# Other slots for batch 0's casts, statistics, transposes, value products and gMLP steps in a block-sparse attention + gMLP kernel

## The chip, the core and the metric

The kernel runs on one core of a Trainium2 chip. The metric is device time in microseconds of one execution, the median over runs. Five engines work side by side and wait for each other through semaphores: PE (matmuls and transposes), ACT (ScalarE), DVE (VectorE), POOL (GpSimd) and SP, which here only issues DMA transfers. Each engine runs its own instructions strictly in the order of the program.

## What is computed

Attention of 4 batches, 8 heads, 768 positions, head size 64, under a block mask (blocks of 32: neighbours, first and last block, three sampled blocks for each block row), and then a gated MLP over the 512 joined head outputs:

```python
scores = scale * np.matmul(q, k.transpose(0, 1, 3, 2))
scores = np.where(mask, scores, -1000000000.0)
attn = np.exp(scores - np.max(scores, axis=-1, keepdims=True))
attn = attn / (np.sum(attn, axis=-1, keepdims=True) + 1e-09)
x = np.matmul(attn, v)            # joined over heads: (4, 768, 512)
h = np.maximum(x @ w_in, 0.0)     # (4, 768, 1024)
u, v = h[..., :512], h[..., 512:]
v_n = (v - mean(v)) / np.sqrt(var(v) + 1e-06)
v_s = np.einsum('ts,bsd->btd', w_spatial, v_n) + b_spatial[None, :, None]
out = (u * v_s) @ w_out           # (4, 768, 512)
```

## The kernel before

**Slots.** The order of work on every engine is the order of the program, and the program is a loop over slots `s` (L838), written out by hand through tables. In each slot PE first computes one group of scores, and ACT takes the exponential of it into `a_all`. Then come the value products that are due, the functions entered for this slot with `when` (the list `early`, L844 and L850), a number of gMLP matmuls taken from a queue (`run_queue`, by the table `STEPS`, L769 to L772), the functions in `late`, and the statistics in `post` (L853 to L856). Scores have two PSUM buffers, so the group of slot s waits for the exponential of slot s - 2.

**Batch 0 (slots 0 to 35).** Heads go in pairs p = 0 to 3. Each unit u = 0 to 11 (`UNITS`, L422) is a third of the query positions of a pair, or of one head of pair 0 over two thirds, and takes three slots. A score group is four matmuls of 256 columns (L441) and one exponential of 1024 (L446); the value products are three groups e = 0, 1, 2 of eight matmuls (L487), by default in slots 3u+3, 3u+4, 3u+5, with exceptions in `AV_AT` (L832). After the third, `normalize` divides on DVE (`rc`, `xn`, L469 and L470), and `xtr_third` (L527) transposes the result on PE into the same PSUM bank and copies it to `xt` on DVE (L525), by default in slot 3u+7 with exceptions in `XT_AT` (L742).

**Queries and keys.** They are loaded as float32 on SP's queue (`load`), cast to bfloat16 on POOL (`cast`, L136), and in batch 0 transposed on PE into `kq`: `tr_first` (keys and the first third of the queries), `tr_rest` (the other queries), `third` and `second` for pair 0; copies from PSUM go through DVE (L217). `rows` copies mask rows on DVE (L247). Pairs 4 to 15 are transposed by DMA instead (`tr_dma`, L412) into `tt`, and two DVE copies (`split`, L416), one for each head, bring them into `kq`. In slots 36 on, a score group is two matmuls of 384 columns (L454) with an exponential of 768 (L458), and six value matmuls (L505) follow it.

**Weights.** The halves of `moe_w_in` are loaded in eight pieces `w_in_load(u, g)` (u = 0 is the half that gives v, u = 1 the one that gives u) and cast on POOL (`w_in_cast`, L233), interleaved by hand with the casts of queries, keys and values (L329 to L357).

**gMLP.** A v product is four matmuls (L579) with a relu (DVE, L609) and then `norm`: statistics on DVE (L612, L613) and, when a group is complete, the inverse deviation on POOL (L616, L618). A later DVE instruction normalizes (L633), due some steps after. A u product has its relu on DVE in batch 0, on ACT after (L638 to L641). Then come six s products (with `w_spt`), gated on DVE (L647), transposed by DMA, and six o products, copied to `osb` by DVE or ACT (L674, L675) and written out. The products of batches 0 to 2 share two PSUM banks (`moe_tag`), which `tr_first`, `tr_rest` and `xtr_pe` use too: a product can begin when the one before the last is copied out.

```python
qk_unit(*divmod(s, 3))                 # L840, slots below 36
early = at.get(s, [])                  # L844
for u, e in av_at.get(s, []):
    av_unit(u, e)
for f in early:                        # L850
    f()
run_queue(STEPS.get(s))
for f in late.get(s, []):              # L853
    f()
while post:
    post.pop(0)()
```

Of the kernel before, what the change touches and what calls it, by code (L numbers as in the profile page):

```python
# [26 lines left out]
def kernel(  # L27
# [38 lines left out]
    S0 = NT * NG * 3  # L66
    FILL, FILL2, FILL3 = 24, 4, 4

    const = ctx.enter_context(tc.tile_pool(name="const", bufs=1))
# [144 lines left out]
    PL, DV = nc.gpsimd, nc.vector  # L214
# [48 lines left out]
    load(1, "q", cs=C25)  # L263
    w_in_load(0, 0)
    cast(0, "q", PL, H1, C03)
# [5 lines left out]
    cast(0, "v", PL)  # L271
    load(3, "v")


# [55 lines left out]
    load(2, "q", cs=C25)  # L330
    w_in_load(0, 2)
    w_in_load(0, 3)
    load(3, "q", cs=C25)
    w_in_load(1, 0)
    w_in_load(1, 1)
    load(0, "q", cs=C45)
    cast(3, "k", PL)
# [4 lines left out]
    cast(2, "v", PL)  # L342
    cast(1, "q", PL, cs=C25)
    cast(3, "v", PL)
    w_in_cast(0, 1, PL)
    w_in_cast(0, 0, PL)
    w_in_load(1, 3)
    w_in_load(1, 2)
# [4 lines left out]
    w_in_cast(1, 0, PL)  # L353
    w_in_cast(1, 1, PL)
    cast(0, "q", PL, cs=C45)
    w_in_cast(1, 3, PL)
    w_in_cast(1, 2, PL)  # L357

# [213 lines left out]
    def product(n, lhs, rhs, last, done, w=512):  # L572
# [11 lines left out]
        return out  # L584

    VN_AGE, VN_STEP = 9, 2
    post = []

    class Moe:
# [14 lines left out]
        def v_product(self, tcc, grp):  # L604
            def done(ps):
                if self.last:
                    nc.scalar.activation(out=self.vn[:, tcc, :], in_=ps, func=AF.Relu)  # L607
                else:
                    ts(self.vn[:, tcc, :], ps, 0.0, ALU.max)  # L609
                def norm():  # L610
                    stats = work.tile([128, 6], FP32, tag="stats", bufs=2)
                    nc.vector.bn_stats(out=stats, in_=self.vn[:, tcc, :])  # L612
                    nc.vector.bn_aggr(out=self.mv[:, tcc, :], in_=stats)  # L613
                    if tcc % grp == grp - 1:
                        cs = slice(tcc - grp + 1, tcc + 1)
                        nc.gpsimd.tensor_scalar(out=self.std[:, cs], in0=self.mv[:, cs, 1],  # L616
                                                scalar1=1e-6, scalar2=None, op0=ALU.add)
                        nc.gpsimd.tensor_tensor(out=self.rstd[:, cs], in0=self.std[:, cs],  # L618
                                                in1=mhalf[:, cs], op=ALU.pow)
                        self.vn_due.extend((t, self.steps + VN_AGE + VN_STEP * i)  # L620
                                           for i, t in enumerate(range(cs.start, cs.stop)))
                if self.last:
                    norm()
                else:
                    post.append(norm)
# [10 lines left out]
        def u_product(self, tcc):  # L636
            def done(ps):
                if self.b == 0:  # L638
                    ts(self.un[:, tcc, :], ps, 0.0, ALU.max)
                else:  # L640
                    nc.scalar.activation(out=self.un[:, tcc, :], in_=ps, func=AF.Relu)  # L641
# [21 lines left out]
        def o_product(self, tcc):  # L663
# [4 lines left out]
            for i in range(parts):  # L668
                cs = slice(i * w, (i + 1) * w)

                def done(ps, i=i, cs=cs):
                    if i == 0:
                        osb["t"] = work.tile([128, DM], FP32, tag="osb", bufs=6, name="osb")
                    on_act = (tcc + i) % 2 == 0 and (self.last or self.b > 0)  # L674
                    (act_copy if on_act else dve_copy)(osb["t"][:, cs], ps)  # L675
# [53 lines left out]

    ROWS = [(1, 2, 4, qcols(0)), (1, 2, 3, K_), (3, 3, 4, K_), (4, 4, 6, qcols(0)), (6, 4, 6, K_), (8, 6, 8, qcols(0)), (9, 6, 8, K_)]  # L730
    when(0, second)
    when(1, third)
    when(2, lambda: filler(FILL3, psum.tile([128, 512], FP32, tag=moe_tag(), bufs=1, name="wps")))
    when(4, c(tr_first, 1))
    when(7, c(tr_first, 2))
    when(9, c(tr_first, 3, 0, 4))
    when(10, c(tr_first, 3, 4))
    for sl, h0, h1, cs in ROWS:
        when(sl, c(rows, slice(h0, h1), cs))
    for p, sl in ((1, 11), (2, 16), (3, 18), (0, 21)):  # L740
        when(sl, c(tr_rest, p, 2 if p == 0 else 1))
    XT_AT = {1: 13}  # L742
    for u in range(1, len(UNITS)):
# [25 lines left out]
    when(29, lambda: deal(moe[0].in_steps("v2 v3 u2 u3", TC), 14))  # L769
    STEPS = {20: 1, 21: 2, 22: 1, 23: 1, 24: 2, 25: 1, 26: 1, 27: 2, 28: 1, 29: 1, 30: 1, 31: 1, 32: 2, 33: 1, 34: 1, 35: 1, 36: 1, 37: 0, 38: 1, 39: 2, 40: 2, 41: 2}  # L770
    STEPS.update({s: 2 if (s % 2 == 0) == (s < 67) else 1 for s in range(42, 92)})
    STEPS.update({43: 2, 46: 1})  # L772
    when(42, lambda: deal(moe[0].in_steps("v4 v5 u4 u5", TC) + moe[0].rest_steps(),
# [57 lines left out]
    LAG = 7  # L831
    AV_AT = {0: (5, 5, 6), 1: (6, 8, 8)}  # L832
    av_at = {}
# [54 lines left out]
```

## Time and profile before

| | |
|---|---|
| median of 3 runs | 211.81 us (211.35 to 211.96) |
| the profiled execution | 211.57 us, span of its instructions 209.8 us |
| PE | 203.2 us busy, 97%, 2141 matmuls and transposes |
| ACT | 167.8 us, 80%, 220 instructions |
| DVE | 134.2 us, 64%, 295 |
| POOL | 69.3 us, 33%, 108 |
| DMA | 41.97 MB, mean 200 GB/s |

Rows of a timeline read: start in us from the span's start, time to the end of the row's instructions in us, engine, line of the kernel, operation, what it writes <- what it reads, shapes, count, and in brackets the idle time of the engine before it with what ended it. Groups read: line, engine, operation, count, then busy us, mean ns of one, and idle time before with its releasers. A row of the list of DMA issues ends with the median us from issue to landing.

### The profile page before, as it was taken

How to read it: one execution, taken by the hardware profiler on the slowest of the kernel's cores; microseconds unless marked ns; L12 is line 12 of the kernel's file. 1: busy time of each engine (PE TensorE's matmuls, PEld its weight loads, DVE VectorE, ACT ScalarE, POOL GpSimd, SP SyncE). 2: the span in 40 equal slices, each digit the busy share in tenths (PEclk: the TensorE clock that was granted, in tenths of full speed). 3: DMA queues.
4: the chain of work that ended last, by engine and by line, in shares of the span. 5: the costliest groups of instructions: out<-in, count | busy, mean ns of one | idle time of the engine just before them, and what ended most of it. 6: DMA issues, size and time to landing. Idle time of an engine off the chain costs nothing.

```text
span 209.8 us, 5271 instructions
## 1 busy us (share of the span) xinstructions
PE 203.2 (97%) x2141; PEld 127.8 (61%) x2141; DVE 134.2 (64%) x295; ACT 167.8 (80%) x220; POOL 69.3 (33%) x108
## 2 busy tenths in 40 slices
PE   8898999999999999999999999999999999999992
PEld 6687878756666666655556655666556556544441
DVE  6998585989754536584987455386785433476541
ACT  5899899999999999979998888979999787266021
POOL 5683979665563214033442040131020000013000
PEclk9999999999999999999999999999999999999999
DMA  5999899999999999999981497795101324610266
GB/s 149 346 356 311 269 369 283 285 219 292 258 375 213 266 152 291 237 296 355 207 239 38 100 264 176 230 314 88 38 3 25 63 53 98 228 66 0 50 170 230
DMA packets 64295, 41.97 MB, mean 200 GB/s; under 512 B 45184, under 2 KB 59024, under 8 KB 64272
## 3 DMA queue, kind: packets, MB, share of 16 engines
q1 hardware_dynamic: 63696, 41.06, 76.4%
q10 hardware_dynamic: 576, 0.59, 0.8%
q8 instruction: 16, 0.26, 0.5%
q14 instruction: 7, 0.06, 0.1%
HBM read 24.38 MB, written 6.29 MB: 146 GB/s over the span
## 4 chain that ended last, share of the span: by engine, by line
PE 86%; DVE 6%; DMA 4%; ACT 2%; POOL 1%; issue 0%; ACTq 0%; SPq 0%
PE ps_moe L579 32%; PE ps L454 22%; PE ps_av L505 13%; PE ps_t L579 8%; DMA w_f<-in_moe_w_in_dram 4%; PE ps_sc L579 4%; PE ps L441 3%; DVE kq L217 2%; PE ps_av L487 2%; ACT a_all L446 1%; DVE vn L185 1%; PE wps L179 1%; PE ps L288 1%; DVE stats L612 1%; DVE xn L470 1%; POOL w_in_t L233 1%
## 5 line engine op out<-in xcount | busy, mean ns | idle before, releaser
L458 ACT ACTIVATE a_all<-ps 128x768 bf16<-128x768 f32 x144 | 114.1, 811 | 15.1 <-PE ps L454 7.4
L454 PE MATMUL ps<-kq 88*128 88x384 bf16 x288 | 70.4, 325 | 0.0
L505 PEld LDWEIGHTS <-a_all 128*128 128x128 bf16 x864 | 45.2, 97 | 20.0
L505 PE MATMUL ps_av<-vv,a_all 128*128 128x65 bf16 x864 | 49.8, 193 | 0.0
L454 PEld LDWEIGHTS <-kq 88*128 88x128 bf16 x288 | 28.0, 97 | 30.6 <-issue 0.2
L579 PE MATMUL ps_moe<-w_in_t,xt 128*128 128x512 bf16 x144 | 43.8, 378 | 0.6 <-POOL w_in_t L233 0.6
L446 ACT ACTIVATE a_all<-ps 128x1024 bf16<-128x1024 f32 x36 | 34.5, 1025 | 2.4 <-PE ps L441 2.2
L579 PE MATMUL ps_moe<-vn,w_spt 128*128 128x512 bf16 x108 | 32.7, 377 | 0.0
L136 POOL CAST nat<-st_k 128x768 bf16<-128x768 f32 (+2 forms) x17 | 13.2, 776 | 44.6 <-DMA st_k<-in_k_dram 42.8
L647 DVE SCALAR_TENSOR_TENSOR un<-ps_moe,b_col,un 128x512 bf16<-128x512 f32 x18 | 13.5, 750 | 15.3 <-PE ps_moe L579 14.7
L441 PE MATMUL ps<-kq 88*128 88x256 bf16 (+1 forms) x140 | 21.7, 275 | 1.0 <-DVE kq L217 0.5
L579 PE MATMUL ps_moe<-w_out_t,gt 128*128 128x512 bf16 x72 | 21.5, 378 | 0.0
L616 POOL TENSOR_SCALAR std<-mv 128x3 f32<-128x3 f32 (+1 forms) x9 | 2.1, 238 | 58.1 <-DVE mv L613 43.1
L469 DVE RECIPROCAL rc<-ps_av 128x6 f32<-128x6 f32 (+1 forms) x36 | 6.6, 183 | 21.0 <-PE ps_av L505 20.5
L579 PEld LDWEIGHTS <-xt 128*128 128x128 bf16 x192 | 15.5, 98 | 7.3 <-DVE xt L217 0.2
L470 DVE TENSOR_TENSOR xn<-ps_av,rc 128x384 bf16<-128x384 f32 (+1 forms) x36 | 18.5, 513 | 1.2
L612 DVE BATCH_NORM_STATS2 stats<-vn 128x6 f32<-128x512 bf16 x24 | 16.5, 687 | 1.4 <-ACT vn L607 0.9
L217 DVE COPY kq<-tt 64x1536 bf16<-64x1536 bf16 x24 | 15.6, 650 | 2.5 <-DMA tt<-nat 2.2
L136 POOL CAST vv<-st_v 128x768 bf16<-128x768 f32 x16 | 13.9, 868 | 9.4 <-DMA st_v<-in_v_dram 9.0
L441 PEld LDWEIGHTS <-kq 88*128 88x128 bf16 x140 | 12.6, 97 | 5.7 <-DVE kq L217 1.4
L136 POOL CAST nat<-st_q 128x768 bf16<-128x768 f32 (+2 forms) x21 | 14.2, 680 | 5.2 <-DMA st_q<-in_q_dram 4.9
L579 PEld LDWEIGHTS <-w_spt 128*128 128x128 bf16 x144 | 11.4, 98 | 5.2
(81 smaller groups left out, 205.8 us busy)
## 6 DMA issues: line engine op xcount, KB each, us to landing
st_v<-in_v_dram SPq DMA_DIRECT2D x16, 384.0 KB, 5.5
st_k<-in_k_dram SPq DMA_DIRECT2D x15, 384.0 KB, 3.9
out_dram<-osb SPq DMA_DIRECT2D x22, 256.0 KB, 2.8
st_q<-in_q_dram SPq DMA_DIRECT2D x12, 384.0 KB, 4.6
ws_f<-in_moe_w_spatial_dram SPq DMA_DIRECT2D x6, 384.0 KB, 8.2
w_f<-in_moe_w_in_dram SPq DMA_DIRECT2D x8, 256.0 KB, 7.7
w_f<-in_moe_w_out_dram SPq DMA_DIRECT2D x4, 256.0 KB, 4.0
st_q<-in_q_dram SPq DMA_DIRECT2D x6, 128.0 KB, 4.7
```

The lines of the kernel that those rows point to most:

```text
L136: eng.tensor_copy(out=dst, in_=src)
L217: nc.vector.tensor_copy(out=o, in_=i)
L441: nc.tensor.matmul(out=ps[:, at:at + n * TW], lhsT=kq[:, h, ci * 128:(ci + 1) * 128], rhs=kq[:, h, qcols(t0, n)], start=True, stop=True)
L446: nc.scalar.activation(out=out, in_=ps, func=AF.Exp, scale=0.125)
L454: nc.tensor.matmul(out=ps[:, hf * 512:hf * 512 + HALF], lhsT=kq[:, j % H, ci * 128:(ci + 1) * 128], rhs=kq[:, j % H, S + hf * HALF:S + (hf ...
L458: nc.scalar.activation(out=a_ref["h", j][:, ci, :].rearrange("p (b c) -> p b c", b=2), in_=ps.rearrange("p (b c) -> p b c", b=2)[:, :, 0:H ...
L469: nc.vector.reciprocal(out=rc[:, 0:n], in_=ps[:, :, D:VA])
L470: nc.vector.tensor_tensor(out=out, in0=ps[:, :, 0:D], in1=rc[:, 0:n].to_broadcast([128, n, D]), op=ALU.mult)
L505: nc.tensor.matmul(out=av_ref[j][:, qc, 0:VA], lhsT=a_ref["h", j][:, ci, qc * 128:(qc + 1) * 128], rhs=vv[p % NVV][:, h, ci, 0:VA], start= ...
L579: nc.tensor.matmul(out=ref["ps"][:, 0:w], lhsT=lhs(i), rhs=rhs(i), start=(i == 0), stop=(i == n - 1))
L612: nc.vector.bn_stats(out=stats, in_=self.vn[:, tcc, :])
L647: nc.vector.scalar_tensor_tensor(out=self.un[:, tcc, :], in0=ps, scalar=b_col[:, tcc:tcc + 1], in1=self.un[:, tcc, :], op0=ALU.add, op1=AL ...
```

## The change

Nothing of the arithmetic changes; instructions move in the program's order, and two evictions move from DVE to ACT.

- The first weight piece (v half, g = 0) is loaded after pair 3's values instead of before, and cast ahead of them, instead of behind them and the next piece. The last queries of pair 0 are loaded before the fourth weight piece, and the pieces (1, 2) and (1, 3) change places around their cast.
- The statistics of v0 and v1 are emitted at the end of slot 23, those of v2 and v3 at the end of slot 36 (`NORM_AT`), instead of in the slot of their product; the normalization is due 8 steps after instead of 9 in batch 0.
- The relu of u3 and the copy of output 4 of batch 0 go to ACT (`U_DVE`, `O_ACT`).
- Pair 1's first transposes are split over slots 3 and 4, pair 3's are joined in slot 10, pair 2's last go from slot 16 to 15; mask rows of pair 3 from slot 8 to 7; `xtr_third` of units 1, 3, 5 and 11 and the value products of units 2, 3, 4, 7, 8 and 10 move by up to one slot (`XT_AT`, `AV_AT`).
- `STEPS` is a new table for slots 20 to 91 with the same total.
- The DMA transpose of pair 5 moves one slot later, the second head's copy of pair 4 one slot sooner (32 instead of 33), and the casts for pairs 7 to 15 one slot later in the program.

```diff
+    U_DVE = (0, 1, 2, 4, 5)
...
     load(1, "q", cs=C25)
-    w_in_load(0, 0)
     cast(0, "q", PL, H1, C03)
...
     load(3, "v")
+    w_in_load(0, 0)
...
     w_in_load(0, 2)
+    load(0, "q", cs=C45)
     w_in_load(0, 3)
     load(3, "q", cs=C25)
     w_in_load(1, 0)
     w_in_load(1, 1)
-    load(0, "q", cs=C45)
...
     cast(1, "q", PL, cs=C25)
+    w_in_cast(0, 0, PL)
+    w_in_load(1, 3)
     cast(3, "v", PL)
     w_in_cast(0, 1, PL)
-    w_in_cast(0, 0, PL)
-    w_in_load(1, 3)
     w_in_load(1, 2)
...
     w_in_cast(1, 1, PL)
+    w_in_cast(1, 2, PL)
     cast(0, "q", PL, cs=C45)
     w_in_cast(1, 3, PL)
-    w_in_cast(1, 2, PL)
...
+    NORM_AT = {1: 23, 0: 23, 3: 36, 2: 36}
+    O_ACT = [(4,), (0, 2, 4), (0, 2, 4)]
...
-                        self.vn_due.extend((t, self.steps + VN_AGE + VN_STEP * i)
+                        self.vn_due.extend((t, self.steps + (8 if self.b == 0 else VN_AGE) + VN_STEP * i)
...
                 if self.last:
                     norm()
+                elif self.b == 0 and tcc in NORM_AT:
+                    late.setdefault(NORM_AT[tcc], []).append(norm)
                 else:
                     post.append(norm)
...
-                if self.b == 0:
+                if self.b == 0 and tcc in U_DVE:
                     ts(self.un[:, tcc, :], ps, 0.0, ALU.max)
...
-                    on_act = (tcc + i) % 2 == 0 and (self.last or self.b > 0)
+                    on_act = (tcc + i) % 2 == 0 if self.last else tcc in O_ACT[self.b]
...
-    ROWS = [..., (8, 6, 8, qcols(0)), (9, 6, 8, K_)]
+    ROWS = [..., (7, 6, 8, qcols(0)), (9, 6, 8, K_)]
...
-    when(4, c(tr_first, 1))
+    when(3, c(tr_first, 1, 0, 4))
+    when(4, c(tr_first, 1, 4))
     when(7, c(tr_first, 2))
-    when(9, c(tr_first, 3, 0, 4))
-    when(10, c(tr_first, 3, 4))
+    when(10, c(tr_first, 3))
...
-    for p, sl in ((1, 11), (2, 16), (3, 18), (0, 21)):
+    for p, sl in ((1, 11), (2, 15), (3, 18), (0, 21)):
         when(sl, c(tr_rest, p, 2 if p == 0 else 1))
-    XT_AT = {1: 13}
+    XT_AT = {1: 12, 3: 17, 5: 23, 11: 41}
...
-    STEPS = {20: 1, 21: 2, 22: 1, 23: 1, 24: 2, 25: 1, 26: 1, 27: 2, 28: 1, 29: 1, 30: 1, 31: 1, 32: 2, 33: 1, 34: 1, 35: 1, 36: 1, 37: 0, 38: 1, 39: 2, 40: 2, 41: 2}
-    STEPS.update({s: 2 if (s % 2 == 0) == (s < 67) else 1 for s in range(42, 92)})
-    STEPS.update({43: 2, 46: 1})
+    STEPS = {20: 0, 21: 3, 22: 2, 23: 0, 24: 2, 25: 1, 26: 2, 27: 2, 28: 0, 29: 1, 30: 1, 31: 1, 32: 2, 33: 1, 34: 1, 35: 1, 36: 1, 37: 0, 38: 1, 39: 2, 40: 2, 41: 2, 42: 1, 43: 3, 44: 3, 45: 0, 46: 2, 47: 1, 48: 2, 49: 1, 50: 2, 51: 0, 52: 2, 53: 1, 54: 1, 55: 1, 56: 2, 57: 3, 58: 1, 59: 1, 60: 2, 61: 2, 62: 3, 63: 1, 64: 1, 65: 1, 66: 1, 67: 2, 68: 3, 69: 1, 70: 1, 71: 1, 72: 1, 73: 2, 74: 2, 75: 1, 76: 1, 77: 3, 78: 1, 79: 1, 80: 1, 81: 2, 82: 0, 83: 3, 84: 1, 85: 2, 86: 0, 87: 2, 88: 2, 89: 3, 90: 1, 91: 1}
...
-        when({4: 18, 5: 26, 6: 38}.get(p, g - 25),
+        when({4: 18, 5: 26, 6: 38}.get(p, g - 24),
              c(cast, p, "k", PL), c(cast, p, "q", PL), c(cast, p, "v", PL))
-        when({4: 20, 5: 30}.get(p, g - 20), c(tr_dma, p))
-        when(g - (7 if p in (9, 13) else 5), c(split, p, 0))
-        when(g - 3, c(split, p, 1))
+        when({4: 20, 5: 31}.get(p, g - 20), c(tr_dma, p))
+        when(31 if p == 4 else g - (7 if p in (9, 13) else 5), c(split, p, 0))
+        when(32 if p == 4 else g - 3, c(split, p, 1))
...
-    AV_AT = {0: (5, 5, 6), 1: (6, 8, 8)}
+    AV_AT = {0: (5, 5, 6), 1: (6, 8, 8), 2: (9, 9, 11), 3: (13, 14, 14), 4: (15, 16, 16), 7: (25, 26, 26), 8: (28, 28, 29), 10: (34, 34, 35)}
```

More of the change, by code (lines that the diff above doesn't have):

```diff
@@ L728, in c @@
         return lambda: f(*a, **kw)
-    ROWS = [(1, 2, 4, qcols(0)), (1, 2, 3, K_), (3, 3, 4, K_), (4, 4, 6, qcols(0)), (6, 4, 6, K_), (8, 6, 8, qcols(0)), (9, 6, 8, K_)]
+    ROWS = [(1, 2, 4, qcols(0)), (1, 2, 3, K_), (3, 3, 4, K_), (4, 4, 6, qcols(0)), (6, 4, 6, K_), (7, 6, 8, qcols(0)), (9, 6, 8, K_)]
     when(0, second)
```

## The prediction

> **What bounds the kernel now.** I read the page's span and its group of exponentials first, then busy time by stage, then the order of time on TensorE (PE) wherever its rows do not follow each other at their usual distance.
>
> ```profile
> span 209.8 us, 5271 instructions
> ...
> L446 ACT ACTIVATE a_all<-ps 128x1024 bf16<-128x1024 f32 x36 | 34.5, 1025 | 2.4 <-PE ps L441 2.2
> ```
>
> ```profile
> 6.00:20.30 14.30, 13.39 (x203) 11.36 (x202) 13.38 (x33) 13.89 (x15) 8.23 (x17) 1.00 1.08 337
> 20.30:43.00 22.70, 21.73 (x308) 17.15 (x305) 16.67 (x43) 21.22 (x23) 17.84 (x23) 1.00 1.08 299
> 43.00:89.00 46.00, 46.00 (x517) 28.65 (x516) 28.71 (x58) 42.46 (x57) 20.09 (x25) 1.00 1.13 258
> 89.00:176.00 87.00, 86.98 (x900) 52.09 (x897) 54.31 (x107) 75.41 (x102) 17.17 (x23) 1.00 0.62 153
> ```
>
> The columns are the stretch, its length, busy time of PE, weight loads, DVE, ACT and POOL, then clock, DMA share and GB/s. Up to 20.3 us (slots 0 to 14) ACT is the bound, 13.89 of 14.30: 36 exponentials of 1024 columns cover 34.5 us, 0.96 each. From 20.3 us PE has more work per slot than ACT, and from 43 us it has no gap. Its matmuls follow at fixed distances, which this piece of PE's timeline shows:
>
> ```profile
> 27.11 0.59 PE L579 MATMUL ps_moe<-w_in_t,xt 128*128 128x512 bf16 x2
> 27.54 0.60 PE L441 MATMUL ps<-kq 88*128 88x256 bf16 x4
> 27.98 0.41 PE L487 MATMUL ps_av<-vv,a_all 128*128 128x65 bf16 x8
> 28.22 0.38 PE L579 MATMUL ps_moe<-w_in_t,xt 128*128 128x512 bf16 x1
> 28.79 0.27 PE L288 MATMUL ps_av<-ident,xn 128*128 128x128 bf16 x2 [0.20 <-DVE kq L217]
> 28.90 0.27 PE L441 MATMUL ps<-kq 88*128 88x256 bf16 x1
> ```
>
> From start to start: two gMLP matmuls 0.43, so 0.215 each; four score matmuls 0.44; eight value matmuls 0.24; two transposes 0.11. The matmul at 28.22 has 0.57 behind it instead of 0.215: PE stood 0.36, of which its row calls only 0.20 idle, because ends are modelled. So I count waits from starts. The change computes the same matmuls, and from slot 92 on the work is dealt as before; its time is that of before, less PE waits that go, plus those that come.
>
> **The opening, slots 15 to 29: +0.06.** Two waits stand here. One is that at 28.22; its cause on DVE:
>
> ```profile
> 27.36 0.69 DVE L612 BATCH_NORM_STATS2 stats<-vn 128x6 f32<-128x512 bf16 x1
> ...
> 28.18 0.56 DVE L217 COPY kq<-ps_av 64x256 bf16<-64x256 bf16 x2
> ```
>
> The copies of pair 0's last queries, at 28.18, stand behind the statistics of v0, begun 0.82 before, and the transposes at 28.79 need their bank. With the statistics after slot 23 the copies come about 0.8 sooner, and that wait of 0.36 goes. The other wait is the first in-projection:
>
> ```profile
> 18.44 0.83 POOL L136 CAST vv<-st_v 128x768 bf16<-128x768 f32 x1 [2.98 <-DMA st_v<-in_v_dram]
> ```
>
> ```profile
> 19.90 1.17 POOL L233 CAST w_in_t<-w_f 128x512 bf16<-128x512 f32 x2 [0.64 <-DMA w_f<-in_moe_w_in_dram]
> 20.09 0.41 PE L487 MATMUL ps_av<-vv,a_all 128*128 128x65 bf16 x8
> 21.02 0.61 POOL L136 CAST nat<-st_q 128x512 bf16<-128x512 f32 x1
> 21.13 0.38 PE L579 MATMUL ps_moe<-w_in_t,xt 128*128 128x512 bf16 x1 [0.63 <-POOL w_in_t L233]
> 22.02 0.39 PE L288 MATMUL ps<-ident,nat 128*128 128x128 bf16 x4
> ```
>
> PE ends its eight value matmuls at 20.33 and waits 0.80 for the second of POOL's two weight casts. The change casts that weight ahead of pair 3's values, so this wait goes. But it also moves pair 2's last transposes, here at 22.02, from slot 16 to slot 15, ahead of that first in-projection matmul. They need the query cast that now begins at 21.02, and that cast needs a transfer:
>
> ```profile
> 8.81 0.51 SPq L227 DMA_DIRECT2D w_f<-in_moe_w_in_dram  x1
> 10.03 0.37 SPq L108 DMA_DIRECT2D st_v<-in_v_dram  x1
> ...
> 12.70 0.66 SPq L108 DMA_DIRECT2D st_q<-in_q_dram  x1
> ```
>
> ```profile
> w_f<-in_moe_w_in_dram SPq DMA_DIRECT2D x1, 256.0 KB, 8.2
> ```
>
> ```profile
> st_q<-in_q_dram SPq DMA_DIRECT2D x1, 256.0 KB, 7.9
> ```
>
> (Issues on SP's queue, and from issue to landing those of 8.81 and 12.70.) The queries land at 12.70 + 7.9 = 20.6. The change swaps the first two issues and leaves the bytes ahead of the queries, so I keep 20.6. POOL's order becomes first weight, values, second weight (lands 19.9, cast to 20.5), queries: 20.64 to 21.25. PE resumes at 21.31, on the transposes, where it resumed at 21.13: 0.18 later, with the same work done. So the wait is not removed, it is handed from a weight to the queries. After that slots 17 to 20 hold 0.44 of scores, 0.24 of values and one step or two transposes, some 0.90 against 0.96 of an exponential; I estimate 0.27 of waits for ACT in slots 18 to 25, where before had 0.03. Sum: 0.18 + 0.27 - 0.03 - 0.36 = +0.06. Bounds: if the queries land so early that nothing waits, 1.0 less; if the first weight, now issued behind the values, lands only with the second (19.9), then weight 0.61, values 0.83, weight 0.61 and queries 0.61 end at 22.4 (casts in a row overlap by 0.05, as the two in 1.17 show), and PE resumes 1.16 later than forecast. Between them the landing read from the row is nearest.
>
> The earlier edits (pair 1's first transposes in slots 3 and 4, mask rows of pair 3 in slot 7, pair 3's transposes in one go, values of unit 2 in slots 9 to 11) shorten at most this:
>
> ```profile
> PE ps L441 <- DVE kq L217: 0.5, 2, 0.3
> ```
>
> I cost them at nothing: whatever PE is ahead at slot 15 ends in the wait for the queries. If that cover goes, they give up to 0.25 (one of the two waits). The other edits up to slot 29 are in the 0.06: before has dealt 12 steps by the end of slot 28, and so has the change. The load of pair 0's last queries goes ahead of a weight on SP's queue and its cast behind one on POOL; PE wants it at 27.0, when POOL is some 0.3 ahead.
>
> **Slot 36: -0.30.**
>
> ```profile
> 39.62 0.83 POOL L136 CAST nat<-st_q 128x768 bf16<-128x768 f32 x1
> 40.81 0.83 POOL L136 CAST vv<-st_v 128x768 bf16<-128x768 f32 x1 [0.37 <-DMA st_v<-in_v_dram]
> ```
>
> ```profile
> 39.91 0.69 DVE L612 BATCH_NORM_STATS2 stats<-vn 128x6 f32<-128x512 bf16 x1
> ...
> 40.84 1.22 DVE L217 COPY kq<-tt 64x1536 bf16<-64x1536 bf16 x1
> 41.98 0.28 DVE L217 COPY xt<-ps_av 128x256 bf16<-128x256 bf16 x1
> ```
>
> ```profile
> 41.67 0.49 PE L454 MATMUL ps<-kq 88*128 88x384 bf16 x2
> ...
> 42.30 0.40 PE L487 MATMUL ps_av<-vv,a_all 128*128 128x65 bf16 x8
> ```
>
> Two score matmuls of 384 columns take 0.33 (0.32 in the rows of slot 92 below), so PE was ready at 42.00 and stood 0.30 for the bank that the copy at 41.98 frees. The change makes the copy of 1.22 one slot sooner and the statistics after slot 36. DVE then does at 39.2 the copy (1.22), the relu of v2 (0.68) and the copy of xt (0.28), and ends at 41.4: no wait. Late next are the statistics of v2 and v3, 0.93 each with their aggregate (39.91 to 40.84); the transposes behind them come only in slot 41. If the cover fails, 0.30 stays. The Trainium skill, "SBUF — State Buffer", section "SBUF: two separate sides", says that VectorE and GpSimd lock a port pair against each other for a whole instruction; the 1.22 beside POOL's cast at 40.81 agrees. By that rule the moved copy could also be held until POOL's cast of 39.62 ends at 40.45 and end at about 41.0; xt would then end at 41.96, just in time, and the sum stays.
>
> **Slot 92: -0.18.**
>
> ```profile
> 88.24 0.56 DVE L470 TENSOR_TENSOR xn<-ps_av,rc 128x384 bf16<-128x384 f32 x1
> 88.43 0.49 PE L454 MATMUL ps<-kq 88*128 88x384 bf16 x2
> 88.72 0.68 DVE L217 COPY osb<-ps_moe 128x512 f32<-128x512 f32 x1
> 88.75 0.35 PE L505 MATMUL ps_av<-vv,a_all 128*128 128x65 bf16 x6
> 88.94 0.50 PE L288 MATMUL ps<-ident,xn 128*128 128x128 bf16 x6
> 89.45 0.59 PE L579 MATMUL ps_moe<-w_in_t,xt 128*128 128x512 bf16 x2
> ```
>
> Six transposes at 0.055 end at 89.27; PE waits 0.18 for the copy at 88.72. Batch 0's output 4 moves to ACT, which takes a copy of 0.68 from in front of these: the wait goes.
>
> **What ACT gets: +0.11.**
>
> ```profile
> L641 ACT ACTIVATE un<-ps_moe 128x512 bf16<-128x512 f32 x12 | 7.1, 594 | 0.0
> ```
>
> Each moved eviction costs ACT about 0.594 (a relu; the copy has the same shape). The relu of u3 falls between the exponentials of slots 41 and 42; slots 43 and 44 have three steps each (0.32 + 0.19 + 0.645 = 1.16 of PE time against 42.46 / 57 = 0.745 of an exponential in the third stretch) and absorb most; I estimate 0.11 of PE wait at slot 44 (bounds 0 and 0.594). The output copy falls into slot 89, also with three steps: 0 (up to 0.594 without that cover). The new table of steps moves at most two steps by some slots; any two neighbouring slots from 42 to 91 keep at least two, 2 x (0.32 + 0.19) + 0.43 = 1.45 of PE. ACT, busy 42.46 of 46.00, has 3.5 in hand over that stretch and covers it: 0, and up to 0.2, one step, for each of the four slots with none otherwise. The later casts for pairs 7 to 15 cost nothing, as POOL is busy 17.17 of 87 us there and waits for loads; if not, a copy from tt comes later on DVE.
>
> **Sum.** 0.06 - 0.30 - 0.18 + 0.11 = -0.31. The profiled execution took 211.57 (span 209.8 and 1.77 around it), which gives 211.26; the median, 0.24 above that execution, goes from 211.81 to 211.5.
>
> **Rivals.** *The opening wait goes as well:* the queries land sooner, or their cast ends before PE arrives at about 20.3. For it: POOL is idle before 19.90. Against it: landing read at 20.6. Then 0.9 more is gained: 210.6. *The cast put first blocks POOL:* the first weight is issued behind the values, and POOL, in order, holds values, second weight and queries behind it. From a landing at 18.6 each microsecond costs one; from 18.92 the change loses, and at 19.85 PE resumes 1.16 later: 211.5 + 1.16 = 212.66. For it: issue at about 10.5 plus 8.2 is 18.7; against it: the two transfers landed by 18.4 together. The Trainium skill, "DMA: Bandwidth & Descriptors", section "Queues, rings and completion order", says that completion on one issuer's queue is not in order of issue; no row here contradicts it, and it leaves this landing open. *The change doesn't do what it says:* waits removed at 41.98 and 89.27 return at the next bank or on ACT (0.594 twice at most), and the time stays at 211.8.
>
> **How the numbers follow.** A measurement of this kernel can tell about 0.3% (0.64 us). Forecast 0.42, opening gone 0.26, POOL blocked 0.16, nothing won 0.16. Faster by over 0.3%: 0.27, nearly all the second case; slower: 0.16; within: 0.57. The range leaves out the far ends of the two outer cases: 210.7 to 212.3; the forecast's own is 211.1 to 211.9.
>
> **What would show it.** In the changed profile: PE starts pair 2's last transposes in slot 15 about 1.0 after its value matmuls, released by POOL's query cast (right), or at once, or later than 21.6 (a rival). No DVE wait before the transposes of slot 23; no wait at the first value matmuls of slot 36; none after the six transposes of slot 92; PE waits of 0.1 behind the relu on ACT. I am wrong if PE's waits from 20 to 43 us change by over 0.6 in sum, or if new ones stand between 43 and 89 us.

## The result and the profile after

| | before | after |
|---|---|---|
| median of 22 runs each, same chip | 211.86 us (211.26 to 213.58) | 211.21 us (210.67 to 212.15) |
| ratio of the runs, 95% interval | | 0.997 (0.9955 to 0.9984) |
| profiled execution, its span | 211.57, 209.8 us | 210.80, 208.9 us |

The change takes 0.65 us off the median. That is at the bound of what a measurement of this kernel can tell from no change, but the interval leaves 1 out. From the first start on PE to the end of the last instruction that computes (ACT's last copy, at 206.59 before and 205.89 after) it is 0.70 us less in the two traces; the span is 0.89 less, the rest lying behind that copy. The page after, and the same four stretches as before (length, then busy PE, weight loads, DVE, ACT, POOL, clock, DMA share, GB/s):

```profile
span 208.9 us, 5273 instructions
```

```profile
6.00:20.30 14.30, 12.99 (x195) 10.83 (x195) 12.87 (x31) 13.58 (x15) 10.08 (x22) 1.00 1.07 337
20.30:43.00 22.70, 22.51 (x323) 17.87 (x321) 16.88 (x43) 21.33 (x24) 18.04 (x23) 1.00 1.13 320
43.00:89.00 46.00, 46.00 (x511) 28.60 (x510) 28.10 (x58) 42.79 (x58) 19.40 (x25) 1.00 1.11 260
89.00:176.00 87.00, 87.00 (x899) 52.13 (x898) 53.32 (x106) 75.44 (x103) 17.29 (x23) 1.00 0.61 147
```

In the first stretch PE and ACT are now less busy than before (12.99 for 13.39, 13.58 for 13.89): the change does not win there, it loses. In the second PE is busy 22.51 of 22.70, where it was 21.73. That stretch holds nearly the whole gain. Its first wait, on the timeline after (start, time to the end, engine, line, operation, count, idle time before):

```profile
20.32 0.41 PE L488 MATMUL ps_av<-vv,a_all 128*128 128x65 bf16 x8
20.92 0.40 PE L289 MATMUL ps<-ident,nat 128*128 128x128 bf16 x4 [0.19 <-POOL nat L137]
...
18.36 0.61 POOL L234 CAST w_in_t<-w_f 128x512 bf16<-128x512 f32 x1 [2.72 <-DMA w_f<-in_moe_w_in_dram]
18.92 0.83 POOL L137 CAST vv<-st_v 128x768 bf16<-128x768 f32 x1
19.69 0.61 POOL L234 CAST w_in_t<-w_f 128x512 bf16<-128x512 f32 x1
20.25 0.61 POOL L137 CAST nat<-st_q 128x512 bf16<-128x512 f32 x1
```

```profile
st_q<-in_q_dram SPq DMA_DIRECT2D x1, 256.0 KB, 7.1
```

The eight value products end at 20.57 (20.32 + 0.24, from starts as the prediction counts), and PE stands 0.35 for POOL's query cast, 20.25 to 20.86. The wait of 0.79 for a weight has become one of 0.35 for the queries. They landed 7.1 us after their issue at 12.81 (last row, the DMA issues of that moment), at 19.9. Their cast did not wait for that: POOL's four casts follow each other without a gap from 18.36, where the first weight has come, to 20.86.

A new wait stands earlier, at slot 12:

```profile
16.10 0.39 PE L289 MATMUL ps<-ident,nat 128*128 128x128 bf16 x4
17.18 0.61 PE L442 MATMUL ps<-kq 88*128 88x256 bf16 x4 [0.69 <-ACT a_all L447]
17.90 0.40 PE L289 MATMUL ps<-ident,xn 128*128 128x128 bf16 x4
...
14.29 0.88 DVE L248 COPY kq<-kq 24x512 bf16<-24x512 bf16 x1
15.20 0.18 DVE L470 RECIPROCAL rc<-ps_av 128x4 f32<-128x4 f32 x1
15.42 0.42 DVE L471 TENSOR_TENSOR xn<-ps_av,rc 128x256 bf16<-128x256 f32 x1
15.85 0.55 DVE L248 COPY kq<-kq 24x1536 bf16<-24x1536 bf16 x1
16.44 1.41 DVE L218 COPY kq<-ps 64x1024 bf16<-64x1024 bf16 x2
...
14.20 0.83 POOL L137 CAST vv<-st_v 128x768 bf16<-128x768 f32 x1 [0.23 <-DMA st_v<-in_v_dram]
```

Four transposes take 0.22, so PE could go on at 16.32 and stood 0.86 until 17.18, and again 0.28 (17.18 + 0.44 to 17.90). The row names ACT, but ACT's exponential had ended at 17.16 and stood idle itself after that; the scores read the copies of pair 3's first transposes, the first of which is begun at 16.44 on DVE, takes 0.68 and ends at 17.12. DVE has no gap over 0.05 in these rows.

Further on the waits that the prediction speaks of are gone or there as follows:

```profile
40.62 0.29 DVE L218 COPY xt<-ps_av 128x256 bf16<-128x256 bf16 x1 [0.42 <-PE ps_av L289]
...
41.32 0.49 PE L455 MATMUL ps<-kq 88*128 88x384 bf16 x2
...
41.65 0.41 PE L488 MATMUL ps_av<-vv,a_all 128*128 128x65 bf16 x8
...
88.02 0.69 DVE L218 COPY osb<-ps_moe 128x512 f32<-128x512 f32 x1 [0.21 <-PE ps_moe L580]
...
88.28 0.49 PE L289 MATMUL ps<-ident,xn 128*128 128x128 bf16 x6
88.76 0.59 PE L580 MATMUL ps_moe<-w_in_t,xt 128*128 128x512 bf16 x2
```

Slot 36 (41.32 to 41.65, 0.33 for two score matmuls) has no wait. Slot 92 still has: six transposes from 88.28 take 0.33, and the next product starts at 88.76, 0.16 late (by unrounded starts).

### The profile page after: what moved, and what is told of

Its sections match the earlier page's. It is cut to its first block, busy times and chain, and to the rows that moved or that the text cites. A ratio compares the mean times of both kernels' runs of the same rounds, so it can differ in the third digit from the quotient of the medians.

```text
span 208.9 us, 5273 instructions
## 1 busy us (share of the span) xinstructions
PE 202.7 (97%) x2141; PEld 127.4 (61%) x2141; DVE 132.4 (63%) x293; ACT 167.4 (80%) x222; POOL 70.3 (34%) x108
## 4 chain that ended last, share of the span: by engine, by line
PE 88%; DMA 6%; POOL 2%; SPq 1%; issue 0%; ACT 0%; ACTq 0%
PE ps_moe L580 34%; PE ps L455 23%; PE ps_av L506 13%; PE ps_t L580 8%; PE ps L442 4%; DMA w_f<-in_moe_w_in_dram 4%; PE ps_sc L580 4%; PE ps_av L488 3%; DMA st_v<-in_v_dram 3%; SPq L109 1%; POOL vv L137 1%; PE ps L289 1%; POOL w_in_t L234 1%; PE ps_av L289 0%; POOL nat L137 0%
## 5 line engine op out<-in xcount | busy, mean ns | idle before, releaser
L580 PE MATMUL ps_moe<-w_in_t,xt 128*128 128x512 bf16 x144 | 43.2, 378 | 0.0
L137 POOL CAST nat<-st_k 128x768 bf16<-128x768 f32 (+2 forms) x17 | 13.9, 815 | 39.6 <-DMA st_k<-in_k_dram 39.6
L471 DVE TENSOR_TENSOR xn<-ps_av,rc 128x384 bf16<-128x384 f32 (+1 forms) x36 | 18.5, 513 | 1.2
L137 POOL CAST nat<-st_q 128x768 bf16<-128x768 f32 (+2 forms) x21 | 14.8, 710 | 5.2 <-DMA st_q<-in_q_dram 4.9
```

What stands on the lines that cost most here:

```text
L137: eng.tensor_copy(out=dst, in_=src)
L471: nc.vector.tensor_tensor(out=out, in0=ps[:, :, 0:D], in1=rc[:, 0:n].to_broadcast([128, n, D]), op=ALU.mult)
L580: nc.tensor.matmul(out=ref["ps"][:, 0:w], lhsT=lhs(i), rhs=rhs(i), start=(i == 0), stop=(i == n - 1))
```

## The experiments

Each kernel was profiled once and timed in 12 runs, beside runs of the kernel before on the same chip. Medians of kernels that differ little scatter by 0.2 us or more (a ratio below is not the quotient of the two medians beside it), so most verdicts are read from the traces. The ten kernels below that differ from the changed one in one to three edits, some of which undo a part of it, came to ratios of 0.9964 to 1.0001, on the mean 0.9984, or 0.33 us; the 0.65 may lie on the lucky side. For that the table below takes the start times of ACT's exponentials, one for each slot, and gives their differences in us: "15-17" is the start of the exponential of slot 17 less that of slot 15. Slots 30 to 33 take 3.02 in all fourteen traces.

| trace | to 5 | 5-15 | 15-17 | 17-21 | 21-30 | 33-37 | 37-60 | 60-92 |
|---|---|---|---|---|---|---|---|---|
| before | 10.63 | 9.76 | 2.82 | 3.80 | 9.53 | 3.72 | 18.81 | 26.86 |
| before, second trace (d2) | 11.78 | 9.52 | 2.05 | 3.80 | 9.53 | 4.33 | 18.81 | 26.86 |
| before, first weight's cast first (c2) | 10.57 | 10.14 | 2.05 | 3.80 | 9.53 | 3.80 | 18.81 | 26.86 |
| after | 10.55 | 10.06 | 2.54 | 3.63 | 9.41 | 3.46 | 18.76 | 26.86 |
| a1, transposes in slot 16 | 10.43 | 9.95 | 2.18 | 4.06 | 9.39 | 3.46 | 18.76 | 26.86 |
| a2, rows in slot 8 | 11.71 | 9.99 | 2.17 | 3.63 | 9.71 | 3.46 | 18.77 | 26.86 |
| a3, both | 11.53 | 10.06 | 2.18 | 4.06 | 9.38 | 3.46 | 18.76 | 26.86 |
| a4, a1 and two halves | 11.62 | 9.81 | 2.18 | 4.06 | 9.38 | 3.46 | 18.76 | 26.86 |
| c3, queries first | 10.93 | 10.08 | 2.17 | 3.63 | 9.41 | 3.46 | 18.77 | 26.86 |
| b1, statistics of v0, v1 at once | 11.62 | 9.59 | 2.17 | 3.63 | 9.76 | 3.46 | 18.76 | 26.86 |
| b2, statistics of v2, v3 at once | 11.78 | 9.48 | 2.17 | 3.63 | 9.40 | 3.46 | 18.76 | 26.86 |
| b3, copy in slot 33 | 10.91 | 9.48 | 2.74 | 3.63 | 9.41 | 3.46 | 18.76 | 26.86 |
| c1, evictions on DVE | 11.94 | 9.88 | 2.17 | 3.63 | 9.41 | 3.46 | 18.82 | 26.86 |
| d1, queries first, rows on POOL | 11.70 | 9.59 | 2.17 | 3.63 | 9.41 | 3.46 | 18.77 | 26.86 |

The first column falls in two kinds, 10.4 to 10.9 and 11.5 to 11.9, whatever the kernel: TensorE comes to full rate early or late (last section). Where it is late, the exponential of slot 15 comes 0.9 us later on the mean (21.45 for 20.58, the first two columns added), and PE finds every load landed.

**a1, pair 2's last transposes back in slot 16.**

```diff
-    for p, sl in ((1, 11), (2, 15), (3, 18), (0, 21)):
+    for p, sl in ((1, 11), (2, 16), (3, 18), (0, 21)):
```

> The changed kernel with pair 2's last transposes back in slot 16; all else as changed. Theory (the wait for the weight was handed to the queries): the wait of 0.35 us before these transposes at 20.57 goes, since the first weight's cast ends at 18.98 and nothing else is late there; the wait of 0.86 before the scores of slot 12 stays. Time 0.3 to 0.4 us under the changed kernel's, 210.85. Rival (something else behind them, such as the bank of scores or an exponential, holds PE there too): the wait only changes its name, time within 0.15 of the changed kernel's.

211.38 us against 211.64 (ratio 1.0001, 0.9981 to 1.0021). The wait at slot 15 is gone, but slots 17 to 21 take 4.06 in place of 3.63:

```profile
21.48 0.39 PE L289 MATMUL ps<-ident,nat 128*128 128x128 bf16 x4
...
22.36 0.28 PE L289 MATMUL ps_av<-ident,xn 128*128 128x128 bf16 x2
22.70 0.61 PE L442 MATMUL ps<-kq 88*128 88x256 bf16 x4
23.48 0.40 PE L488 MATMUL ps_av<-vv,a_all 128*128 128x65 bf16 x8 [0.17 <-DVE xt L218]
```

Two transposes take 0.11, so the scores at 22.70 are 0.23 late: they wait for the copies of the very transposes that were moved. The values at 23.48 are 0.34 late, for `xt` behind those copies on DVE. The rival held: the wait changed its name. The wait of 0.86 at slot 12 was 0.27 here, though nothing in slots 0 to 14 differs from the changed kernel. So it was partly chance. Where nothing waits at slot 15 (late full rate), slots 15 to 21 take 6.24 with the transposes in slot 16 (a3, a4) and 5.80 with them in slot 15 (b2, c1): within the changed kernel this move is worth 0.44.

**a2, a3, a4: what made the wait at slot 12.** a2 puts the mask rows of pair 3 back to slot 8; a3 does that and a1; a4 is a1 with pair 3's transposes in two halves.

```diff
-    ROWS = [..., (7, 6, 8, qcols(0)), (9, 6, 8, K_)]
+    ROWS = [..., (8, 6, 8, qcols(0)), (9, 6, 8, K_)]
```

```diff
-    when(10, c(tr_first, 3))
+    when(9, c(tr_first, 3, 0, 4))
+    when(10, c(tr_first, 3, 4))
```

> The changed kernel with the mask rows of pair 3's queries back in slot 8, so that DVE's copy of 24x512 comes behind the reciprocal and product of slot 11's values, not ahead of them; all else as changed. Theory 1 (slot 12 waits for DVE's queue, and that copy took 875 ns beside POOL's cast where it takes 285 alone): the copy runs later and short, DVE is at pair 3's copies about 0.65 sooner (16.45), the waits before the scores and the transposes of slot 12 fall from 0.86 + 0.28 to about 0.2 + 0.28. Theory 2 (the query cast ending at 20.86 is the cover): the time stays within 0.15 of the changed kernel's all the same, and the wait for that cast grows by 0.65, from 0.35 to about 1.0. Rival to 1 (joining pair 3's transposes made the wait): slot 12 waits as before, 1.1. Rival to 2: the time falls by 0.65.

> Both edits of the two runs before: pair 2's last transposes in slot 16 and pair 3's mask rows in slot 8. Theories 1 and 2: without the cover both waits go, 0.35 + 0.65 = 1.0 under the changed kernel, 210.2; the query cast is just reached, with a wait of at most 0.2 in slot 16. Rival (the opening is bound by the loads, which the casts follow): the wait for the query cast comes back in slot 16 with 0.5 or more, time 210.7 or above.

> The changed kernel with pair 2's last transposes in slot 16 and pair 3's first transposes in two halves again (slots 9 and 10). DVE's order of work is the same as with the transposes joined. Theory 1 (slot 12 waits for DVE's queue): its waits stay at 0.86 + 0.28, time as with the last transposes in slot 16 alone, 210.85. Rival (joining the transposes made that wait): the waits fall to those of the kernel before, 0.16, and the time to about 210.0.

Measured 211.24, 211.35 and 211.68 against 211.64 (ratios 0.9986, 0.9992, 1.0000, all intervals with 1 in them). At slot 12 PE waited 0.15 + 0.28 in a2, 0.16 + 0.28 in a3, 0.26 + 0.28 in a4. That looks like theory 1, but a2 and a3 gave it back in slots 6 and 9 (0.35 + 0.42 and 0.40 + 0.42 before their scores), and over slots 5 to 15 they took 9.99 and 10.06, like the change itself. Joining the transposes is not it either: a4 waits as a1 does. One thing that differs between traces is which of two engines comes first. In the changed kernel DVE's copy of 24x512, of its rows above, took 875 ns beside POOL's casts; the same copy in a1 took 286:

```profile
14.65 0.29 DVE L248 COPY kq<-kq 24x512 bf16<-24x512 bf16 x1
...
12.89 1.88 POOL L137 CAST vv<-st_v 128x768 bf16<-128x768 f32 x2 [0.35 <-DMA st_v<-in_v_dram]
14.71 0.69 POOL L137 CAST nat<-st_q 128x512 bf16<-128x512 f32 x1
```

In a1 the copy began 0.1 before POOL's second cast ended; in the changed kernel 0.1 after one of 0.83 had begun (14.20). In the kernels whose program in slots 0 to 14 is the changed one's (after, a1, b1, b2, b3, c1), slots 5 to 15 took 9.48 to 10.06, mean 9.74; with the old program (before, d2, c2) 9.52 to 10.14, mean 9.81. The early edits are worth nothing that these traces can tell. a2, a3 and a4 came to full rate late, so they could not show the cover of theory 2. a2 also took 9.71 in slots 21 to 30: PE waited 0.29 before the transposes of slot 23 for POOL's cast of pair 0's last queries (27.30 to 27.70), which the change put behind a weight's cast; that weight came late (26.74, POOL idle 2.28 before it). The prediction saw POOL 0.3 ahead there; in this execution it was not.

**c2: the kernel before with the first weight's cast put first.**

```diff
+    w_in_cast(0, 0, PL)
+    w_in_load(1, 3)
     cast(3, "v", PL)
     w_in_cast(0, 1, PL)
-    w_in_cast(0, 0, PL)
-    w_in_load(1, 3)
```

> The kernel before with one edit of the change alone: POOL casts the first weight ahead of pair 3's values. Executions differ in when TensorE's matmuls come to full rate (at 3.7 to 5.1 us in three of the six traces so far, at 9.0 to 9.5 in the others, and then slot 15 is 0.8 to 1.1 later and waits for no load), so the opening is read from a trace of the first kind. Theory (the cast's place in POOL's order is the whole of the old wait): the wait of 0.79 before the first in-projection goes; PE reaches pair 2's last transposes in slot 16 at 21.2 and waits there for the query cast (21.02 to 21.63 before), 0.4; gain 0.4 in such a trace, 0 in the other kind, 0.1 to 0.3 in the median. Rival (the wait is for landings, whatever the order): the same 0.8 stands before the transposes, gain 0.

211.38 against 211.93 (ratio 0.9976, 0.9956 to 0.9996), early full rate. Slots 15 to 17 take 2.05 in place of 2.82: there is no wait for the weight, and the queries, cast 20.05 to 20.67, were in time for slot 16.

```profile
20.40 0.41 PE L487 MATMUL ps_av<-vv,a_all 128*128 128x65 bf16 x8
...
17.93 0.83 POOL L136 CAST vv<-st_v 128x768 bf16<-128x768 f32 x1 [0.88 <-DMA st_v<-in_v_dram]
19.34 0.61 POOL L233 CAST w_in_t<-w_f 128x512 bf16<-128x512 f32 x1 [0.58 <-DMA w_f<-in_moe_w_in_dram]
```

But this execution cannot tell the theory from its rival. The second weight, cast from 19.90 before, had come by 19.34 here, and PE was at slot 15 0.31 later (20.40 for 20.09). In the old order the two weights would have been cast from 19.34 to 20.51 (an estimate, with the 1.17 that two took before), and PE was ready for the first in-projection only at 20.64: no wait in that order either. The same estimate from the landings of the second weight in the changed kernel's own trace (19.13), in a1 (18.83) and in b3 (18.98) ends at 20.0 to 20.3, each time before PE has done the value products of slot 15 (20.57, 20.33, 20.34). The old wait of 0.79 stands in one trace, whose second weight landed 7.7 us after its issue; in the eleven others with that place in the order it took 6.5 to 7.2. By the timings c2 is faster than the kernel before, with an interval that hardly leaves 1 out. That the moved cast gives the opening's gain is not shown.

**c3: queries ahead of the second weight.**

```diff
+    load(2, "q", cs=C25)
     w_in_load(0, 1)
-    load(2, "q", cs=C25)
...
+    cast(2, "q", PL, cs=C25)
     w_in_cast(0, 1, PL)
     w_in_load(1, 2)
-    cast(2, "q", PL, cs=C25)
```

> The changed kernel with pair 2's last queries loaded and cast ahead of the second weight. Theory (in an execution of early full rate the opening waits for that query cast alone): the cast ends about 0.5 to 0.7 sooner and the wait of 0.35 before the transposes of slot 15 goes; the second weight, wanted in slot 16, is cast by 21.0 and delays nothing; 0.3 gained in such an execution, none in one of late full rate, 0.1 to 0.2 in the median. Rival (the queries' place in the load order does not move their landing, or the weight is late next): a wait of 0.3 or more stands at slot 15 or 16 in an execution of early full rate.

211.05 against 211.93 (ratio 0.9975, 0.9952 to 0.9998). The cast ends at 19.79, and PE, which was 0.4 later here than in the changed kernel, goes straight on:

```profile
19.17 0.61 POOL L137 CAST nat<-st_q 128x512 bf16<-128x512 f32 x1
...
20.72 0.41 PE L488 MATMUL ps_av<-vv,a_all 128*128 128x65 bf16 x8
20.96 0.39 PE L289 MATMUL ps<-ident,nat 128*128 128x128 bf16 x4
```

Slots 15 to 17 take 2.17, as wherever the new order finds its loads landed, and nothing is late behind. A cast ended at 19.79 would have been in time for the changed kernel's PE too, ready at 20.57. By the timings this version is as fast as the changed kernel; a lead of some 0.1 us can't be told. The 0.3 expected of such an execution is not in the trace (span 209.0 for 208.9), as PE came later by more than the wait that went.

**b1, b2: the statistics at once.**

```diff
-    NORM_AT = {1: 23, 0: 23, 3: 36, 2: 36}
+    NORM_AT = {3: 36, 2: 36}                 # b1
+    NORM_AT = {1: 23, 0: 23}                 # b2
```

> The changed kernel with the statistics of v0 and v1 taken at once again, not after slot 23. Theory: they stand ahead of the copies of pair 0's last queries (at 27.2 in the changed kernel) by 0.69 + 0.2, and PE waits 0.3 to 0.4 before the transposes of slot 23, as before; time 0.3 to 0.4 over the changed kernel's. Rival (the other edits around slot 23 removed that wait): no wait there, time as the changed kernel's.

> The changed kernel with the statistics of v2 and v3 taken at once, not after slot 36; the copy of pair 4's transposed tile stays one slot sooner. Theory (the copy, moved out of the way, is what frees slot 36): the copy of xt comes at 41.1 in place of 40.6, and PE waits at most 0.15 before the values of slot 36; time within 0.2 of the changed kernel's. Rival (the statistics made that wait): 0.3 before these values.

b1: 211.42 against 211.93 (0.9984, 0.9963 to 1.0005). Slots 21 to 30 take 9.76 in place of 9.41, so the later statistics are worth 0.35, but not at the place that the theory named:

```profile
30.55 0.60 PE L442 MATMUL ps<-kq 88*128 88x256 bf16 x4
31.35 0.40 PE L488 MATMUL ps_av<-vv,a_all 128*128 128x65 bf16 x8 [0.20 <-DVE xt L218]
...
29.66 0.69 DVE L615 BATCH_NORM_STATS2 stats<-vn 128x6 f32<-128x512 bf16 x1
...
31.02 0.28 DVE L218 COPY xt<-ps_av 128x256 bf16<-128x256 bf16 x1
```

PE is ready at 30.99 and waits 0.36 for `xt`, which stands behind the statistics of v1. There is no wait at slot 23. b2: 211.46 (0.9983, 0.9957 to 1.0008), slots 33 to 37 at 3.46: the statistics of v2 and v3 cost nothing where the copy is early.

**b3: the second copy of pair 4 in slot 33.**

```diff
-        when(32 if p == 4 else g - 3, c(split, p, 1))
+        when(g - 3, c(split, p, 1))
```

> The changed kernel with the second copy of pair 4's transposed tile one slot later again (slot 33), behind the relu of v2; the statistics stay after slot 36. Theory (the wait of slot 36 came from that copy's 1.22 us beside POOL's cast): in the changed kernel POOL's cast of 128x768 runs at 39.4 to 40.3, so the copy, begun at 39.8, is held to about 40.3 and ends at 40.5 to 40.9; xt follows by 41.2, and PE, ready at 41.3, waits 0 to 0.15. Rival (the copy's slot alone makes the wait, wherever POOL is): 0.3 before the values of slot 36.

211.20 against 211.77 (0.9964, 0.9942 to 0.9987); slots 33 to 37 at 3.46, no wait.

```profile
39.28 0.83 POOL L137 CAST vv<-st_v 128x768 bf16<-128x768 f32 x1
...
39.81 0.70 DVE L218 COPY kq<-tt 64x1536 bf16<-64x1536 bf16 x1
40.61 0.29 DVE L218 COPY xt<-ps_av 128x256 bf16<-128x256 bf16 x1
...
20.10 0.41 PE L488 MATMUL ps_av<-vv,a_all 128*128 128x65 bf16 x8
20.90 0.40 PE L289 MATMUL ps<-ident,nat 128*128 128x128 bf16 x4 [0.40 <-POOL nat L137]
```

With the statistics late, the copy may stand in either slot; with the copy early, the statistics may (b2). Either alone frees slot 36; both undone together weren't tried. The last two rows show the cover that a2 could not: in this execution PE was at slot 15 0.22 earlier than in the changed kernel's trace, having waited less at slot 12, and it waited 0.56 in place of 0.35 and went on at 20.90 in place of 20.92.

**c1: relu of u3 and output copies back on DVE.**

```diff
-    U_DVE = (0, 1, 2, 4, 5)
+    U_DVE = (0, 1, 2, 3, 4, 5)
-    O_ACT = [(4,), (0, 2, 4), (0, 2, 4)]
+    O_ACT = [(), (0, 2, 4), (0, 2, 4)]
```

> The changed kernel with the relu of u3 and batch 0's output copies on DVE again. Theory (the wait after the six transposes of slot 92 is that copy's own distance from the last product, 0.08 + 0.69, and not the copy ahead of it): it is 0.16 to 0.18 here too; ACT's two pieces cost PE nothing where they were, so the time stays within 0.1 of the changed kernel's, but for up to 0.3 if the relu of 0.68 delays the copy of xt behind it. Rival (as predicted: 0.18 won at slot 92, 0.11 lost by the relu): slot 92 waits 0.18 where the changed kernel has 0, and the time rises by 0.07.

211.28 against 211.77 (0.9978, 0.9952 to 1.0004). Slots 37 to 60 take 18.82 for 18.76, so the relu on ACT wins 0.06 and costs PE nothing. Slots 60 to 92 are 26.86 either way, and slot 92 waits 0.16 here as in the changed kernel.

**d1: c3, and the mask rows of pair 3's queries on POOL.**

```diff
-    ROWS = [..., (7, 6, 8, qcols(0)), (9, 6, 8, K_)]
+    ROWS = [..., (9, 6, 8, K_)]
...
     cast(1, "q", PL, cs=C25)
+    rows(slice(6, 8), qcols(0), PL)
     w_in_cast(0, 0, PL)
```

(with c3's edits)

> The changed kernel with pair 2's last queries loaded and cast ahead of the second weight (the run of that edit alone gave 211.05), and the mask rows of pair 3's queries copied by POOL, behind its cast of pair 1's queries, in place of DVE. Theory (slots 5 to 12 wait for DVE's queue): DVE has 0.29 to 0.88 less to do there, PE's waits before the scores and transposes of slot 12 fall to under 0.4 in sum, the time falls by 0 to 0.3 against the changed kernel. Rival (the copies of two further pieces and the exponentials bound these slots, or POOL's copy meets DVE's): the waits stay at 0.5 to 1.1, time unchanged.

211.44 against 211.77 (0.9979, 0.9953 to 1.0005). Slot 12 waits 0.07 + 0.26, but slot 9 0.34; slots 5 to 15 take 9.59, inside the range of the unchanged ones. Nothing won that can be told.

**d2: the kernel before, once more.**

> The kernel before, unchanged, for a second trace of it and for the spread of the comparison. Ratio 1.000, give or take 0.002. In any trace PE waits about 0.36 before the transposes of slot 23 and 0.30 before the values of slot 36. If TensorE comes to full rate late (9.0 to 9.6 us), there is no wait of over 0.2 before the first in-projection of slot 15; if early, 0.2 to 0.8, by the landing of the second weight between 18.8 and 19.9.

211.77 against 211.77 (0.9994, 0.9968 to 1.0021): the comparison's own spread. Full rate was late, and there was no wait for the weight at slot 15, as expected. Slot 23 waited 0.36. The other wait was not 0.30 at slot 36 but 0.75 at slot 33 and 0.17 at slot 36:

```profile
39.00 0.60 PE L441 MATMUL ps<-kq 88*128 88x256 bf16 x4
40.19 0.40 PE L487 MATMUL ps_av<-vv,a_all 128*128 128x65 bf16 x8 [0.59 <-DVE xt L217]
...
37.77 1.33 DVE L217 COPY kq<-tt 64x1536 bf16<-64x1536 bf16 x1 [0.51 <-DMA tt<-nat]
39.03 0.91 DVE L185 TENSOR_SCALAR vn<-vn,mv,rstd 128x512 bf16<-128x512 bf16 x1
39.87 0.27 DVE L217 COPY xt<-ps_av 128x256 bf16<-128x256 bf16 x1
...
35.54 3.15 POOL L551 CAST ws_b<-ws_f 128x768 bf16<-128x768 f32 x2
38.97 0.83 POOL L136 CAST nat<-st_k 128x768 bf16<-128x768 f32 x1 [0.28 <-PE ps_av L487]
```

Two DVE pieces in front of `xt` were stretched beside POOL's casts. The old order lost 0.26, 0.34 and 0.87 in slots 33 to 37 against the 3.46 that all eleven traces with the new order show.

## Why the prediction was right or wrong

The 211.21 measured lie inside the range, 0.3 under the forecast of 211.5. Its sum, -0.31, was made for a profiled execution; between the two traces it came to -0.70. The difference of 0.39 is that of one term, while the misses in the others cancel.

By a sign that the prediction set itself it was wrong: PE's waits from 20 to 43 us were to change by no more than 0.6 in sum. Counted from starts they fell by 0.9, from 0.79 + 0.36 + 0.30 and 0.03 for ACT to 0.35 + 0.24; 0.24 of this is only that PE came to the wait of slot 15 later (20.57 for 20.33). By the other sign it held: no new wait stands between 43 and 89 us.

- **Opening, the resumption of PE (+0.18 in the sum): wrong in size.** That the wait passes from the weight to the query cast was right. The failed step is "so I keep 20.6": the queries landed at 19.88, and their cast ended at 20.86, not 21.25. PE went on at 20.92, 0.21 before the old 21.13 instead of 0.18 after, a difference of 0.39, and -0.31 - 0.39 is -0.70. That landing was taken from one row of one execution, 7.9 us after the issue. The ten other traces with that place in the order (all but after, c3, d1 and before itself) have 6.7 to 7.4 and landings from 19.2 to 20.7, so the one row was the longest of all. c2, with the issues in the order of before, landed at 20.0: no change of that order is needed for the earlier landing. With that landing gone as the bound, POOL's chain behind the first weight set the end of the query cast, 18.36 to 20.86 or 2.50 us. That is the mechanism of the rival "The cast put first blocks POOL", at an earlier landing than that rival feared. (The 18.6 and 18.92 given for it do not come out of the prediction's own casts: 0.61 + 0.83 + 0.61 + 0.61 less three overlaps of 0.05 is 2.51, so the chain binds from 21.25 - 2.51 = 18.74, and the change loses from 0.31 later, 19.05.) That the new order of casts, and not the landings of the two executions, won the 0.21 is not shown: by the estimate under c2 the old order would not have waited at slot 15 in the changed kernel's execution. The true opening lies between the forecast and the rival "the opening wait goes as well", and it depends on the execution: where full rate is late nothing waits in either kernel (d2 and b1).
- **Early edits at nothing: right.** Over slots 5 to 15 the profiled pair lost 0.30, in part by the stretched copy of 0.88, and the wait for the query cast covered it, as b3 shows. Without that cover the two orders are alike on the mean.
- **Waits for ACT, 0.27 in slots 18 to 25 against 0.03: right in sum.** Summed from starts between 22.5 and 31 us, the changed kernel's trace has 0.24, of which 0.09 is for `xt` and not for ACT.
- **Statistics after slot 23, -0.36: right in size** (b1: 0.35); only, undone alone, the wait comes at slot 25.
- **Slot 36, -0.30: right,** and shown to be more than that in other executions, up to 0.87 with slot 33. Of the two edits named for it either is enough.
- **Slot 92, -0.18: wrong.** The failed step is "takes a copy of 0.68 from in front of these: the wait goes". The copy that PE waits for begins when its product has ended, at 88.02, and takes 0.69 with or without another ahead of it, to 88.71; PE, which had issued the product by 87.77, is back at its bank after 0.84 of other work, at 88.61. 0.02 was won (0.18 to 0.16).
- **Relu on ACT, +0.11: wrong.** ACT absorbed all of it, and 0.06 was won by what DVE no longer does (c1). The two errors cancel: -0.07 forecast for both, -0.07 measured between 43 and 92 us (0.05 + 0.18 of waits before, 0.16 after). That agreement is luck.
- **New table of steps, later casts: right,** 26.86 for slots 60 to 92 in all traces.

The loss of the rival that POOL would be blocked behind the first weight did not come: that cast began at 18.36, before the 18.92 that the prediction gives (19.05 by its own casts), and at 17.4 to 18.5 in the ten other traces with the new order.

In the table the -0.70 of the profiled pair is -0.08 up to slot 5, +0.02 from 5 to 17, -0.29 from 17 to 30, -0.26 from 33 to 37, -0.05 from 37 to 60 and some 0.03 behind. So up to slot 17 the opening brought nothing in this pair: the 0.28 won at slot 15 went into the 0.30 lost ahead of it. Where nothing waits at slot 15 on either side (d2 against b2, c1 and d1), slots 15 to 30 gain 0.17 (15.38 to 15.21 or 15.20), the later statistics less the new waits for ACT; slots 33 to 37 gain 0.26 to 0.87, and slots 37 to 60 gain 0.05. These pieces are there whatever the opening does, and at 0.5 to 1.1 us together they are enough for the 0.65 measured. The early edits bring nothing that the runs can tell, and whether the first weight's cast put first gains stays open: it would need an execution in which the old order is seen to wait. No version tried is surely faster than the changed kernel.

## What to carry to other kernels

A landing time read from one execution is a sample: where an edit turns on half a microsecond of it, take the spread over several traces before choosing between the outcomes, or put the transfer where it does not matter. A run in which a wait is gone shows that an edit removed it only if, with the landings of that same run, the old order would still have waited. A DVE copy that feeds PE should not stand behind statistics that are wanted much later, and beside a POOL cast it can take more than twice its time. And a bank's wait is removed only by shortening the way from the product's end through its copy, not by clearing the queue in front of a copy that was not waiting there.

## What the hardware showed

**The start of full rate.** In PE's timeline of a2 (first rows) four score matmuls of 256 columns take 0.83 from start to start, 5.38 to 6.21; in the changed kernel (second rows) 0.45, 5.24 to 5.69.

```profile
5.38 1.03 PE L442 MATMUL ps<-kq 88*128 88x256 bf16 x4
6.21 0.31 PE L302 MATMUL ps<-ident,nat 128*128 128x128 bf16 x1
```

```profile
5.24 0.61 PE L442 MATMUL ps<-kq 88*128 88x256 bf16 x4 [0.16 <-DVE kq L218]
5.69 0.22 PE L302 MATMUL ps<-ident,nat 128*128 128x128 bf16 x1
```

TensorE began at half rate in all fourteen traces, and the first matmuls at full spacing came at 3.9 to 5.5 us in six and at 9.2 to 10.1 in eight; the kernel before, run twice, fell once in each kind. The late kind is on the mean 1.0 us behind at slot 5 and 0.6 at slot 17 (columns of the table added). The granted clock shows 1.00 in all of this, so the rate has to be read from spacings. The Trainium skill, "TensorE: Matmul & The Clock Gate", section "Part 1: The HAM clock gate", says that the array starts at half clock and is released after a busy window of about 3.4 us, which runs freely and does not start with the kernel; half rate and a jump between executions agree. It gives the scatter as 0.5 us either way; the traces have two groups some 5 us apart.

**DVE and POOL.** Copies of DVE from SBUF to SBUF took 0.29 to 0.56 alone and up to 1.33 beside a cast of POOL, ending 0.14 to 0.41 after that cast; copies from PSUM were not stretched (0.68 to 0.69 for 64x1024 throughout). The Trainium skill, "SBUF — State Buffer", section "SBUF: two separate sides", says that of a GpSimd instruction and a DVE one in a mode with two ports, whichever starts first holds the shared ports for its whole instruction, and the rows agree. In them a start 0.1 us sooner or later decides over 0.6 us of DVE's time. That is one reason why slots 5 to 15 of one program took 9.48 to 10.06: the two traces with 9.48 have no stretched copy of mask rows there, the changed kernel's has one. It is not shown to be the only one, as c3 took 10.08 with 0.1 us of such stretching.
